# Two mixtures of experts after attention: the held layer in halves, and a phase's comparisons in one step

## The chip, the core and the metric

The kernel runs on one core of a Trainium2 chip. TensorE multiplies, ScalarE and VectorE read its results from PSUM and compute on SBUF, GpSimd does small elementwise work and issues the scatters and gathers by index, and SyncE's queue issues the other DMAs. Each engine runs its own instructions in order and waits for others by semaphores. The metric is device microseconds of one execution, from the runs' median. A profile is of one execution, on the hardware's own clock.

## What is computed

Causal attention with a cumulative bias feeds a first mixture of experts, and this feeds a second one. Cut to the mixtures (N = 1152 tokens, DM = 512, E = 8 experts, hidden width 1024):

```
logits = x @ w_gate                       # first mixture: each token to its best expert
e      = argmax(logits);  gate_w = softmax(logits)[e]
x      = gate_w * (relu(x @ w1[e]) @ w2[e])

logits = x @ w_gate2                      # second mixture: all (token, expert) pairs by falling logit;
for tok, e in descending order:           # a pair counts if the token is free and the expert has room
    if not assigned(tok) and counts[e] < N // E: assign
out[tok of e] = relu(x[tok of e] @ w1b[e]) @ w2b[e]
```

The second mixture's experts hold 144 tokens each. The assignment is found in phases: in each phase every free token points at its best expert that still has room, the kernel ranks the pointing tokens among each other (how many have a larger logit), and an expert that is thereby full closes. The expert that closed in a phase is the next whose weights are loaded.

## The kernel before

**First mixture.** Experts run one after the other, those with few tokens last. Layer 1 of an expert (`layer1`, lines 1004 to 1015) multiplies weights split into a float16 high and a bfloat16 low half with tokens split the same way, three products a term, into PSUM; ScalarE evicts the high half of the hidden values `h`, VectorE subtracts for the low half. Layer 2 follows. Then `back1` turns an expert's results to token rows `xo`, and GpSimd scatters them into `x2d` in HBM.

**The held expert.** The last expert (136 token slots, `HELD`) stops after layer 1. Its contribution to the second mixture's logits comes by a short way (`logits_pe`, `spread_pe`), so that routing can start; its layer 2 is the filler work of TensorE while VectorE routes. It is written as a generator, `held_steps` (from line 1313): each `next` gives 6 matmuls of 136 columns; after the first two of four output blocks (48 matmuls) ScalarE evicts the high half `y` (line 1329), VectorE makes the low half (line 1331), and after the other two (another 48) the same again. Then `rows_steps` transposes both halves of the tokens (line 1348, 16 transposes, 68 tokens a half), ScalarE evicts each (`xo`, `x2f`, line 1350) and GpSimd scatters each (line 1176). `FILL` gives out the steps between the last parts of the first mixture ('f' is a step of the held layer, 'r' one of the rows of the expert before it):

```
FILL = ". rfff rrrff fff"
```

**The first routing phase** is written out by hand behind that. Row maxima `m` are spread over 128 columns by nine transposes (line 1221), evicted by ScalarE as `rowb` (line 1224), and each of nine token tiles is compared with all others (`compare`, a 128 x 1152 comparison): on VectorE (line 1661), or, for the tiles in `act_t`, as a sign on ScalarE (line 1659). TensorE multiplies each comparison with the tiles' expert choice (`products`, line 1667) and so counts ranks. `held_next(n)` takes n steps of the held layer in between:

```
held_next(); ahead(0, 1, 2); held_next(); ahead(4, 3); held_next(8); ahead(5)
held_next(2); ahead(7, 6, 8); head(True); ranked(0, 1, 2, 4, 3); held_next(4); ranked(5, 7, 6, 8)
```

From the ranks VectorE makes `evi` (the number of the first expert that is full, line 1679), for which SyncE's queue waits before it issues that expert's weights (`known`, line 1698, loads at line 128), and `tok` (its token list, line 1715). Then GpSimd gathers that expert's tokens from `x2d` (`gather`, line 1523), which has to wait for all scatters into it. Nine more loads are let go when the gather is issued (`passed`, line 1704). While the weights arrive, ScalarE splits off their high halves (`split_hi`, line 160, `wh`) and VectorE the low ones (`split_lo`, line 164). The tokens left over are packed (line 1804 and the products at line 1806) and the second phase starts. `spread` transposes the gathered tokens (line 1543) and ScalarE and VectorE copy them (line 1548); then layer 1 of the second mixture's first expert begins.

**The second mixture.** Layer 1 has ticks after each group of matmuls and each eviction, layer 2 (`second2`, line 1966) too; a table of scripts says which step of the routing ('w'), which split ('h', 'l'), which half of a gather's spreading or which scatter of results stands at which tick. The generator `phases` yields at each 'w'. In a phase with comparisons (five token tiles, tiles 1 and 4 on ScalarE) one step spreads the row maxima, three steps compare (two tiles each, in the order 0, 2, then 1, 3, then 4), one multiplies and ranks. From the third expert on the first of the three stands at layer 1's first tick and the second at its sixth, so that two evictions (line 1013) and two splits (line 164) of VectorE lie between.

## Time and profile before

| | us |
|---|---|
| median of 3 runs | 436.03 (436.0 to 436.26) |
| profiled execution | 437.73 |
| its span, first to last instruction | 435.9 |
| TensorE busy | 394.1 (90%) |
| VectorE busy | 327.3 (75%) |
| ScalarE busy | 259.1 (59%) |
| GpSimd busy | 189.2 (43%) |
| mean granted TensorE clock | 0.973 |

Busy time is a mean over stages: attention to about 150 us, the first mixture to about 268, the handover with the first routing phase to 297.5, the second mixture behind it. Matmuls are pipelined, so the busy time of one overlaps that of the next; the distance between their starts is their pace. A wait for several semaphores is put down to the one that came last by the profile.

### The profile page before, as it was taken

How to read it: one execution, taken by the hardware profiler on the slowest of the kernel's cores; microseconds unless marked ns; L12 is line 12 of the kernel's file. 1: busy time of each engine (PE TensorE's matmuls, PEld its weight loads, DVE VectorE, ACT ScalarE, POOL GpSimd, SP SyncE). 2: the span in 40 equal slices, each digit the busy share in tenths (PEclk: the TensorE clock that was granted, in tenths of full speed). 3: DMA queues.
4: the chain of work that ended last, by engine and by line, in shares of the span. 5: the costliest groups of instructions: out<-in, count | busy, mean ns of one | idle time of the engine just before them, and what ended most of it. 6: DMA issues, size and time to landing. Idle time of an engine off the chain costs nothing.

```text
span 435.9 us, 13913 instructions
## 1 busy us (share of the span) xinstructions
PE 394.1 (90%) x5359; PEld 365.3 (84%) x5359; DVE 327.3 (75%) x951; ACT 259.1 (59%) x470; POOL 189.2 (43%) x306
## 2 busy tenths in 40 slices
PE   1669999998888799999999999879999999998994
PEld 1447888887767799999999999838999999998993
DVE  7889999989686367868778894776767977977530
ACT  4448888876672356555566742743657695775641
POOL 4387788875870602132044180522043243433131
PEclk9979999999999999999999998968999999999998
DMA  7797989984936989999999390179999797899711
GB/s 145 174 218 182 222 181 212 220 213 147 375 119 201 326 245 321 344 393 344 335 288 384 81 174 5 30 243 312 309 302 378 228 352 267 243 345 284 235 43 36
DMA packets 91327, 103.04 MB, mean 236 GB/s; under 512 B 56136, under 2 KB 59208, under 8 KB 91251
## 3 DMA queue, kind: packets, MB, share of 16 engines
q1 hardware_dynamic: 85859, 91.85, 72.8%
q0 software_dynamic: 4192, 9.91, 7.4%
q8 instruction: 44, 0.72, 0.7%
q10 hardware_dynamic: 1200, 0.30, 0.3%
q14 instruction: 32, 0.26, 0.2%
HBM read 81.42 MB, written 14.59 MB: 220 GB/s over the span
## 4 chain that ended last, share of the span: by engine, by line
PE 57%; DVE 15%; DMA 14%; issue 5%; ACT 3%; POOL 2%; SPq 1%; another core or an unknown queue 1%; POOLq 0%; ACTq 0%; DVEq 0%
PE C L1061 11%; DMA xg<-x2d,tok 8%; PE A L1004 4%; PE A L1006 4%; PE A L1005 4%; PE C L1966 4%; DVE wl L164 4%; PE pog L559 3%; PE pT L452 3%; DMA kf<-in_k_dram 2%; PE pM L476 2%; DVE wf L164 2%; PE A L1966 2%; PE D L1966 2%; DMA wf<-in_moe_w_dram 2%
## 5 line engine op out<-in xcount | busy, mean ns | idle before, releaser
L164 DVE TENSOR_TENSOR wl<-wf,wh 128x1024 bf16<-128x1024 f32 x64 | 78.0, 1233 | 28.6 <-ACT wh L160 27.7
L160 ACT ACTIVATE wh<-wf 128x1024 f16<-128x1024 f32 x64 | 65.8, 1052 | 18.1 <-DMA wf<-in_moe_w_dram 9.7
L1005 PE MATMUL A<-xt,wh 128*128 128x144 f16 (+4 forms) x288 | 61.0, 235 | 0.0
L1006 PE MATMUL A<-xt,wl 128*128 128x144 f16 (+4 forms) x288 | 60.9, 235 | 0.0
L1004 PE MATMUL A<-xt,wh 128*128 128x144 f16 (+4 forms) x288 | 60.9, 235 | 0.0
L1061 PE MATMUL C<-h,wf 128*128 128x160 f32 (+7 forms) x544 | 58.3, 268 | 0.0
L1176 POOL DMA_INDIRECT x2d<-xo,tix x14 | 22.9, 1639 | 74.8 <-DVE l L1193 26.5
L1004 PEld LDWEIGHTS <-wh 128*128 128x128 f16 x512 | 51.0, 100 | 3.3 <-remote 1.7
L1006 PEld LDWEIGHTS <-wl 128*128 128x128 bf16 x512 | 50.9, 99 | 1.9 <-issue 1.7
L1005 PEld LDWEIGHTS <-wh 128*128 128x128 f16 x512 | 50.9, 99 | 0.8 <-issue 0.3
L1990 POOL DMA_INDIRECT out_dram<-x2f,tok x14 | 19.5, 1392 | 54.0 <-ACT h L1012 19.0
L414 POOL TENSOR_TENSOR pl<-pf,ph 128x512 f16<-128x512 f32 x30 | 35.6, 1196 | 10.3 <-DVE ph L403 8.6
L536 ACT ACTIVATE pf<-pE,XB 128x512 f32<-128x512 f32 (+4 forms) x80 | 36.6, 509 | 3.9 <-PE pE L531 3.6
L1061 PEld LDWEIGHTS C<-h,wf 128*128 128x128 f32 x256 | 36.2, 190 | 0.0
L488 DVE CUSTOM_DVE_ANT_0 junk<-pM,cb 128x128 f16<-128x128 f32 (+4 forms) x80 | 32.1, 429 | 4.5 <-PE pM L478 3.8
L164 DVE TENSOR_TENSOR wf<-wf,wf 128x1024 bf16<-128x1024 f32 x28 | 33.4, 1219 | 2.6 <-ACT wf L160 2.6
L1966 PE MATMUL C<-h,wf 128*128 128x144 f16 (+1 forms) x304 | 32.7, 261 | 0.0
L476 PE MATMUL pM<-al,ar 128*128 128x128 f16 (+2 forms) x96 | 26.3, 315 | 7.0 <-DVE rm L488 6.9
L1523 POOL DMA_INDIRECT xg<-x2d,tok x16 | 19.7, 1234 | 24.2 <-DMA x2d<-x2f,tix 6.2
L160 ACT ACTIVATE wf<-wf 128x1024 f16<-128x1024 f32 x28 | 29.3, 1055 | 0.0
L559 PE MATMUL pog<-vf,pf 128*128 128x65 f32 x180 | 28.7, 282 | 0.0
L1004 PE MATMUL C<-xt,wh 128*128 128x144 f16 x128 | 24.6, 226 | 0.0
(431 smaller groups left out, 1180.5 us busy)
## 6 DMA issues: line engine op xcount, KB each, us to landing
wf<-in_moe_w_dram SPq DMA_DIRECT2D x128, 512.0 KB
xd<-zero SPq DMA_DIRECT2D x18, 257.0 KB
cb<-cumd SPq DMA_DIRECT2D x16, 288.0 KB
x2d<-zero SPq DMA_DIRECT2D x9, 260.5 KB
kf<-in_k_dram SPq DMA_DIRECT2D x16, 128.0 KB
vf<-in_v_dram SPq DMA_DIRECT2D x16, 128.0 KB
qf<-in_q_dram SPq DMA_DIRECT2D x14, 128.0 KB
bl<-al SPq DMA_DIRECT2D x16, 72.0 KB
```

The source lines that it names most:

```text
L160: nc.scalar.activation(hi, src, AF.Copy)
L164: nc.vector.tensor_sub(lo, src, hi)
L414: (nc.gpsimd if ENG[name][i % 2] == "P" else nc.vector).tensor_sub(o, x, y)
L476: nc.tensor.matmul(o, AR[m][:, t * P:(t + 1) * P], AL[m][:, j0:j1], start=True, stop=not diag)
L488: nc.vector.tensor_tensor_reduce(junk[:w, :j1 - j0], o, CB[m][:w, j0:j1], 1.0, r if t == 4 and j0 == 0 else -3e38, OP.add, OP.max, r)
L536: nc.scalar.activation(d, o, AF.Exp, bias=x, scale=2.0 ** -13)
L559: nc.tensor.matmul(o, pf[:, c:c + P], VF[n % 4][:, j, h], start=False, stop=j == t)
L1004: nc.tensor.matmul(ph[:, g], wh[:, c, fs], xt[:, c], start=c == 0, stop=False)
L1005: nc.tensor.matmul(ph[:, g], wh[:, c, fs], xt[:, 4 + c], start=False, stop=False)
L1006: nc.tensor.matmul(ph[:, g], wl[:, c, fs], xt[:, c], start=False, stop=c == 3)
L1061: nc.tensor.matmul(py[:, g], a[:, f, d], b[:, f], start=k == 0, stop=k == len(terms) - 1)
L1966: nc.tensor.matmul(py[:, g], a[:, f, d], b[:, f], start=k == 0, stop=k == len(terms) - 1)
```

## The change

The held layer is made in two halves of its tokens instead of two halves of its output blocks. The generator `products` multiplies all four output blocks for 68 tokens, then for the other 68: twice as many matmuls, each with half the columns and 12 to a step instead of 6. High half, low half, the rows' homes in SBUF (`homes`: memset and gate value on GpSimd), the transposes (`turn`) and the copy with its scatter (`put`) are methods that the hand-written order calls one by one. VectorE compares seven of the nine tiles instead of six. In the later phases the three comparisons of VectorE (tiles 0, 2, 3) all stand in the first of the three steps.

```diff
-    def held_steps():
-        for e in HELD:
-            N = CAPS[e]
-            hh, hl = held[e]
-            ys = yh, yl = in_halves(mo1["y"], "y", 4, N)
-            for dp in range(2):
-                py = mo1["py"].tile([P, 2, N], F32)
-                for g in range(2):
-                    wh, wl = split_ws(2 * e)(1, 2 * dp + g)
+    class Held:
+        def __init__(self, e):
+            self.e, self.w = e, CAPS[e] // 2
+            self.ys = in_halves(mo1["y"], "y", 4, CAPS[e])
+            self.py, self.pb, self.xs = {}, {}, []
+        def products(self):
+            hh, hl = held[self.e]
+            for q_ in range(NQ):
+                sl = slice(q_ * self.w, (q_ + 1) * self.w)
+                py = self.py[q_] = mo1["py"].tile([P, 4, self.w], F32)
+                for d in range(4):
+                    wh, wl = split_ws(2 * self.e)(1, d)
                     terms = [x for f in range(8) for x in ((wh, hh, f), (wl, hh, f), (wh, hl, f))]
                     for i, (a, b, f) in enumerate(terms):
-                        nc.tensor.matmul(py[:, g], a[:, f], b[:, f], start=i == 0, stop=i == 23)
-                        if i % 6 == 5:
+                        nc.tensor.matmul(py[:, d], a[:, f], b[:, f, sl], start=i == 0, stop=i == 23)
+                        if i % 12 == 11:
                             yield
-                r = slice(2 * dp, 2 * dp + 2)
-                nc.scalar.activation(yh[:, r], py, AF.Copy, scale=YS)
-                yield
-                nc.vector.scalar_tensor_tensor(yl[:, r], py, YS, yh[:, r], op0=OP.mult, op1=OP.subtract)
-                yield
-            yield from rows_steps(e, ys)
+        def high(self, q_):
+            sl = slice(q_ * self.w, (q_ + 1) * self.w)
+            nc.scalar.activation(self.ys[0][:, :, sl], self.py[q_], AF.Copy, scale=YS)
+        def low(self, q_):
+            sl = slice(q_ * self.w, (q_ + 1) * self.w)
+            nc.vector.scalar_tensor_tensor(self.ys[1][:, :, sl], self.py[q_], YS, self.ys[0][:, :, sl],
+                                           op0=OP.mult, op1=OP.subtract)
+        def homes(self):
+            for q_ in range(NQ):
+                t, g = slots(self.e, q_)
+                xo = mo1["o"].tile([SL, DM + E + 1], F32, name=("xo", "x2f")[q_])[:g.shape[0]]
+                nc.gpsimd.memset(xo[:, DM:DM + E], 0.0)
+                back1_gate(g, xo)
+                self.xs.append((t, xo))
+        def turn(self, q_):
+            pb = self.pb[q_] = pbs.tile([P, 512], F32).bitcast(F16)[:self.w]
+            for k in range(2):
+                for c in range(4):
+                    nc.tensor.transpose(pb[:, (4 * k + c) * P:(4 * k + c + 1) * P],
+                                        self.ys[k][:, c, q_ * self.w:(q_ + 1) * self.w], ident)
+        def put(self, q_):
+            t, xo = self.xs[q_]
+            nc.scalar.activation(xo.bitcast(F16)[:, :2 * DM], self.pb[q_], AF.Copy)
+            back1_out(t, xo)
...
-    head, tiles, compare, products = ranks(pc, m, Bo, Bh0, NTT, (1, 4, 7), 2)
+    head, tiles, compare, products = ranks(pc, m, Bo, Bh0, NTT, (1, 7))
...
-    held_next()
-    ahead(0, 1, 2)
-    held_next()
-    ahead(4, 3)
-    held_next(8)
-    ahead(5)
-    held_next(2)
-    ahead(7, 6, 8)
+    ahead(0)
+    last_held.high(0)
+    last_held.homes()
+    ahead(1)
+    held_next(4)
+    last_held.low(0)
+    ahead(2, 3)
+    last_held.turn(0)
+    last_held.put(0)
+    held_next(4)
+    last_held.high(1)
+    ahead(4)
     head(True)
-    ranked(0, 1, 2, 4, 3)
-    held_next(4)
-    ranked(5, 7, 6, 8)
+    ranked(0, 2, 1)
+    last_held.low(1)
+    ahead(7, 5)
+    last_held.turn(1)
+    last_held.put(1)
+    ranked(3, 4)
+    ahead(6, 8)
+    ranked(7, 5, 6, 8)
...
-                for k in range(3):
-                    gt += [(compare(t), t) for t in tiles[2 * k:2 * k + 2]]
+                for ts in ((0, 2, 3), (1,), (4,)):
+                    gt += [(compare(t), t) for t in ts]
                     yield
```

In the rows of the order below, numbers behind a name tell buffers apart; `g`, `wl_84` and `wh_83` are homes of comparisons, `y` the held layer's result, `m` the row maxima, `mx` the first step after the ranks. VectorE in the first routing phase, before:

```order
L1230 TENSOR_SCALAR Bh_3127<-Bo_3126 128x72
L1661 TENSOR_SCALAR g<-rowb,m_3125 128x1152 x2
L1331 SCALAR_TENSOR_TENSOR y<-C_5155,y 128x2x136
L1661 TENSOR_SCALAR g<-rowb,m_3125 128x1152
L1661 TENSOR_SCALAR wl_84<-rowb,m_3125 128x1152
L1331 SCALAR_TENSOR_TENSOR y<-C_5305,y 128x2x136
L1661 TENSOR_SCALAR wh_83<-rowb,m_3125 128x1152 x2
```

and VectorE in the changed kernel at the same place:

```order
L1230 TENSOR_SCALAR Bh_3127<-Bo_3126 128x72
L1689 TENSOR_SCALAR g<-rowb,m_3125 128x1152
L1339 SCALAR_TENSOR_TENSOR y<-C_5155,y 128x4x68
L1689 TENSOR_SCALAR g<-rowb,m_3125 128x1152 x3
L1339 SCALAR_TENSOR_TENSOR y<-C_5352,y 128x4x68
L1689 TENSOR_SCALAR wl_84<-rowb,m_3125 128x1152
L1689 TENSOR_SCALAR wh_83<-rowb,m_3125 128x1152 x2
```

The first subtraction stands behind one comparison instead of two, there are seven comparisons instead of six, and three instead of two stand behind the second subtraction. ScalarE in the same phase, before (`rowb` ahead, the splitting of weights behind):

```order
L1224 ACTIVATE rowb<-A_5232 128x384
L1329 ACTIVATE y<-C_5155 128x2x136
L1659 ACTIVATE g<-rowb,m_3125 128x1152 x2
L1329 ACTIVATE y<-C_5305 128x2x136
L1659 ACTIVATE wl_84<-rowb,m_3125 128x1152
L1350 ACTIVATE xo<-D_5417 68x1024
L1350 ACTIVATE x2f<-D_5430 68x1024
L160 ACTIVATE wh_83<-wf_78 128x4x256 x2
```

and ScalarE in the changed kernel:

```order
L1224 ACTIVATE rowb<-A_5262 128x384
L1335 ACTIVATE y<-C_5155 128x4x68
L1687 ACTIVATE g<-rowb,m_3125 128x1152
L1359 ACTIVATE xo<-D_5406 68x1024
L1335 ACTIVATE y<-C_5352 128x4x68
L1687 ACTIVATE wl_84<-rowb,m_3125 128x1152
L1359 ACTIVATE x2f<-D_5504 68x1024
L160 ACTIVATE wh_83<-wf_78 128x4x256 x2
```

The first half's rows `xo` moved ahead of the second eviction, and one sign fewer stands between. VectorE at the third expert of the second mixture (`h` the evictions of layer 1, `wf_3047` the low halves of layer 2's weights), before:

```order
L1661 TENSOR_SCALAR g<-rowb,m_6378 128x640 x2
L1013 SCALAR_TENSOR_TENSOR h<-D_6497,h 128x2x144
L164 TENSOR_TENSOR wf_3047<-wf_3038,wf_3047 128x1024 x2
L1013 SCALAR_TENSOR_TENSOR h<-C_6530,h 128x2x144
L1661 TENSOR_SCALAR g<-rowb,m_6378 128x640
```

and in the changed kernel:

```order
L1689 TENSOR_SCALAR g<-rowb,m_6472 128x640 x3
L1013 SCALAR_TENSOR_TENSOR h<-D_6591,h 128x2x144
L164 TENSOR_TENSOR wf_3047<-wf_3038,wf_3047 128x1024 x2
L1013 SCALAR_TENSOR_TENSOR h<-C_6626,h 128x2x144
L1906 TENSOR_REDUCE mx_6750<-px 128x5
```

The third comparison moved ahead of two evictions and two splits; the same holds at the two experts that follow.

## Rows read from the trace of the kernel before

**Rows 1.** Engines by stretch: busy us (instructions), granted clock, DMA share, GB/s.

```profile
core 0: us, PE busy (x) PEld busy (x) DVE busy (x) ACT busy (x) POOL busy (x), PEclk, DMA share, GB/s
289.00:297.50 8.50, 6.12 (x65) 3.58 (x66) 6.36 (x16) 6.73 (x9) 2.32 (x5) 0.70 0.83 257
297.50:331.00 33.50, 33.50 (x445) 33.27 (x444) 24.08 (x99) 17.43 (x30) 10.26 (x14) 0.97 0.99 322
...
296.20:299.60 3.40, 3.40 (x34) 2.85 (x33) 2.86 (x19) 0.64 (x1) 0.50 (x2) 0.50 1.02 361
```

**Rows 2.** Chain of waits in the handover: start, us, what.

```profile
282.69 6.67 DMA x2d<-x2f,tix
...
290.23 4.42 DMA xg<-x2d,tok
```

**Rows 3.** TensorE in time, handover: start, us, line, shapes, count, [idle before, releaser].

```profile
273.37 4.07 PE L1325 MATMUL C<-h,wf 128*128 128x136 f16 x66
...
277.45 0.37 PE L1667 MATMUL A<-Bo,g 128*128 128x8 f16 x9
...
288.85 1.33 PE L1221 MATMUL A<-identf,m 128*128 128x128 f32 x5 [0.86 <-DVE m L1833]
...
294.69 0.43 PE L1543 MATMUL A<-ident,xg 72*128 72x72 f16 x8 [2.38 <-DMA xg<-x2d,tok]
...
297.54 0.33 PE L1004 MATMUL D<-xt,wh 128*128 128x144 f16 x1
```

**Rows 4.** VectorE in time, first routing phase.

```profile
274.33 1.58 DVE L1661 TENSOR_SCALAR g<-rowb,m 128x1152 f16<-128x1152 f32 x2 [1.63 <-ACT rowb L1224]
...
278.08 0.44 DVE L1331 SCALAR_TENSOR_TENSOR y<-C,y 128x272 f16<-128x272 f32 x1 [0.20 <-ACT y L1329]
278.44 1.54 DVE L1661 TENSOR_SCALAR wh<-rowb,m 128x1152 f16<-128x1152 f32 x2
...
284.72 0.16 DVE L1715 TENSOR_SCALAR tok<-s 72x2 int32<-72x2 f32 x1
```

**Rows 5.** ScalarE in time, first routing phase and handover.

```profile
274.99 0.40 ACT L1329 ACTIVATE y<-C 128x272 f16<-128x272 f32 x1 [0.69 <-PE C L1325]
...
280.20 1.01 ACT L1350 ACTIVATE x2f<-D 68x1024 f16<-68x1024 f16 x1
...
290.84 1.06 ACT L160 ACTIVATE wh<-wf 128x1024 f16<-128x1024 f32 x1 [0.46 <-DMA wf<-in_moe_w_dram]
291.80 0.75 ACT L1224 ACTIVATE rowb<-A 128x384 f32<-128x384 f32 x2
...
296.56 0.64 ACT L1548 COPY xt<-A 128x576 f16<-128x576 f16 x1 [0.68 <-PE A L1543]
```

**Rows 6.** SyncE's queue in time: issues of the second mixture's weights.

```profile
283.35 17.12 SPq L128 DMA_DIRECT2D wf<-in_moe_w_dram  x10
```

**Rows 7.** What the DMA moved from 262 to 300 us, 40 slices of 0.95.

```profile
GB/s 1 37 0 0 0 0 17 0 0 0 0 31 127 48 88 9 0 0 0 17 0 0 54 98 199 257 338 345 356 382 276 209 127 169 99 269 405 347 319 375
```

**Rows 8.** TensorE's waits from 296 us: us in total, times, longest.

```profile
PE px L1667 <- DVE g L1661: 1.1, 3, 0.4
```

**Rows 9.** TensorE in time, third and fifth expert of the second mixture.

```profile
339.54 0.27 PE L1667 MATMUL px<-Bh,g 128*128 128x8 f16 x5
340.17 0.28 PE L1667 MATMUL px<-Bo,g 128*128 128x8 f16 x5 [0.36 <-DVE g L1661]
...
374.21 1.94 PE L1966 MATMUL D<-h,wf 128*128 128x144 f16 x20
```

**Rows 10.** VectorE in time, third expert of the second mixture.

```profile
336.57 0.45 DVE L1013 SCALAR_TENSOR_TENSOR h<-D,h 128x288 f16<-128x288 f32 x1
...
339.20 0.45 DVE L1013 SCALAR_TENSOR_TENSOR h<-C,h 128x288 f16<-128x288 f32 x1
339.57 0.55 DVE L1661 TENSOR_SCALAR g<-rowb,m 128x640 f16<-128x640 f32 x1
```

**Rows 11.** ScalarE in time, fifth expert of the second mixture.

```profile
374.83 0.39 ACT L1015 ACTIVATE h<-A 128x288 f32<-128x288 f32 x1
```

More of the change, by code (lines that the diff above doesn't have):

```diff
@@ L1406, in tile_attention_moe_moe @@
     stw.close()
-    todo = {"r": rows_steps(*pend), "f": held_steps(), ".": iter(())}
+    last_held = Held(E - 1)
+    todo = {"r": rows_steps(*pend), "f": last_held.products(), ".": iter(())}
     fill()
```

## The prediction

> **What bounds the kernel now.** I read the stretches by engine first [rows 1]. From 297.5 us to 331 us TensorE is busy in all of its time, so the second mixture of experts is bound by TensorE, and whatever moves the start of its first expert moves the end. From 289 to 297.5 TensorE works 6.12 of 8.5 us: the handover between the two mixtures is where time is lost. Then the chain of waits [rows 2]: the second scatter of the held expert's rows takes 6.67 us to land, and the gather behind it 4.42 us. Then the engines' own order in time. TensorE waits 2.38 us for the gathered rows at 294.69 and begins layer 1 of the first expert at 297.54 [rows 3]. ScalarE converts that expert's weights while they arrive (released by their DMA at 290.84), then makes the row copies at 291.80, and its copy of the gathered tokens at 296.56 waits 0.68 us for TensorE [rows 5]. So two arms meet there: the gather, which ends last, and the weights through ScalarE, which could be 0.68 us later before it decides. Last, TensorE's waits after 297.5 [rows 8]: three waits, 1.1 us in all, for VectorE's third comparison of a phase. One of them is at 340.17; the comparison itself ends at 340.12 because it stands behind two evictions and two weight splits that begin at 336.57 [rows 9, 10].
>
> The profiled execution took 437.73 us with a span of 435.9; the runs' median is 436.03. I make the sum on the span and carry the difference to the median one to one.
>
> **Part 1: the held layer by halves.** It removes 96 matmuls of 136 columns and adds 192 of 68. Now one takes (4.07 - 0.17)/65 = 60 ns [rows 3]; 0.17 is what is left of a single one, from 0.27 for five and 0.37 for nine, which gives 25 ns each [rows 3, 9]. For 68 columns with new weights each time the nearest rows are 8 columns, 25 ns, and the transposes of 72 columns, (0.43 - 0.17)/7 = 37 ns. I take 33, between them and nearer to 72. That is 6.3 us for 5.8: 0.5 us more, half of it in the first half.
>
> The Trainium skill, TensorE: Matmul & The Clock Gate, section Back-to-back issue gap, gives about 81 ns for a sustained pair of weight load and matmul at 128 columns; its section on LDWEIGHTS counts columns over 1.2, so 107 ns for 128. By either, halving the columns would halve nothing and the sum would be that of rival (d). The trace does not agree: 60 ns at 136 columns, 25 ns at 8 with new weights each time [rows 3].
>
> What this does to VectorE decides. Now ScalarE's eviction of the first 48 products starts at 274.99 [rows 5], 0.6 after the 48th matmul (273.37 + 17 x 0.06). VectorE runs six comparisons and two subtractions from 274.33 and ends the last pair at 278.44 + 1.54 = 279.98 [rows 4]. In the changed order it has seven comparisons (ScalarE gives one up) and two stops:
> - first comparison 274.4 to 275.2; the eviction of half one starts about 0.2 later than now, 275.2 + 0.40; the subtraction 0.44, to 276.05;
> - three comparisons at 0.78 (1.58/2), to 278.4. Then it waits: half two needs 96 x 33 ns = 3.2 us of TensorE after 274.7 and the eight transposes of half one, 0.5 us, which stand in between; 278.4, and 0.6 to the eviction: 279.0;
> - eviction 0.40, subtraction 0.44, three comparisons: 282.2.
>
> So the last comparison comes about **2.0 us later** (282.2 - 279.98 = 2.2 with 33 ns, 1.8 with 31), and with it all that follows on VectorE: the expert's number, for which the queue of the weights waits, the token list, now ready at 284.88 [rows 4], and the compaction. The row maxima's transposes, now done at 288.85 + 1.33 = 290.2 [rows 3], come at 292.2.
>
> *The gather.* Half one's rows can be scattered near 279.7, but half two's transposes wait for the subtraction at 279.85; 0.5 of transposes, 0.3 to ScalarE and 1.0 of eviction make 281.6, where now the second eviction ends at 280.20 + 1.01 = 281.2 [rows 5]. The second scatter therefore starts near 282.5, where it is now (282.69). What is gained is its landing: now it shares the DMA engines with the weights from 283.35 on [rows 6], in the change these come 2.0 later. Between the same 6.67 and 1.3 less (the share of the weights, below) the gather starts 0 to 1.3 earlier and its rows are there at 293.4 to 294.7. The token list (286.9) is not in its way. This arm is no later than now.
>
> *The weights.* They are asked for 2.0 later, at 285.35. Upper bound: they land 2.0 later. Lower bound: in the three slices from 283.85 the DMA moved 98, 199 and 257 GB/s, where it reaches 350 after them [rows 7]; without the scatter those slices give back (252 + 151 + 93)/350 x 0.95 = 1.35 us, leaving 0.65. Between them lies the gather, which now comes after the weights and in the change runs among them: 0.3 MB, 0.9 us at 350 GB/s, of which the middle of the range has half. I take 1.3. ScalarE has 0.68 us in hand, so layer 1 starts **0.6 us later** (0 to 1.3). The second scatter's early queueing helps no more than this.
>
> The memsets and gates of the two halves on GpSimd stand behind VectorE's first comparisons as now; ScalarE's copy of half one needs them, and cover is there until 279.0, when the second eviction would be due anyway.
>
> **Part 2: the comparisons in the first step.** Phases 1 to 3 keep VectorE's order, since no other VectorE work lies between their steps. In phases 4, 5 and 6 the third comparison moves ahead of two evictions and two splits: 0.45 us later for these, and TensorE no longer waits. What a wait costs: without it the next product would start 0.025 after the fifth at 339.54 + 0.10 = 339.64, so at 339.67 instead of 340.17, 0.50 us [rows 9]; the row's own 0.36 is the lower figure. Next late is the second layer's low half, which the eviction moved from 339.65 to 340.1 gives, needed at about 340.9: covered. In the third of these places ScalarE's last eviction of layer 1 ends at 374.83 + 0.39 = 375.22 behind a weight conversion that waited for its DMA [rows 11], and the matmuls that read it are the last four of the row at 374.21, near 375.5 [rows 9]: only 0.2 to 0.3 is to be had there. So 0.5 + 0.5 + 0.2 = **1.2 us gained** (0.7 for two at 0.36, 1.5 for three at 0.50).
>
> **Sum:** +0.6 - 1.2 = -0.6, 435.4 us.
>
> **The rivals.** (a) *The weights hardly move.* If they land only 0.65 later, ScalarE's slack takes it, layer 1 starts when it does now, and all three waits go: -1.5, 434.5. For it: the slow first slices; against: the gather in their midst. (b) *The weights follow the expert's number wholly*: +1.3 - 1.2, 436.1. For it: the weights' four parts keep the DMA near 350 GB/s to their end. (c) *As much again at half clock, slower than before.* TensorE was granted 0.50, the lower of its two levels, from 296.2 to 299.6, after its pauses, and layer 1 began in it [rows 1]. If the products come thinner and 2.0 later and as much again is granted half, 3.4 us at half pace cost 1.7: -0.6 + 1.7 = +1.1, 437.1. It decides from a start of layer 1 near 298.5 on, when TensorE's pauses last until then. Against it: the filler products of the handover come later too, and so nearer to layer 1. (d) *A matmul costs its weights*, not its columns: 192 at 60 ns put the first half 96 x 27 ns = 2.6 us further behind and the second 5.2, so the last comparison 7.2 later than now; less 0.7 in the landing and 0.7 in hand, and less 1.2, that is +4.6, 440.6. The 25 ns of the products, with new weights each, speak against it.
>
> That the change does not do what it says can be left aside: the order shows the halves and the moved comparison.
>
> **How the numbers follow.** Forecast 0.40, own range 434.8 to 436.0, three tenths of it under 435.16. (a) 0.28, (b) 0.16, (c) 0.13, (d) 0.03. A measurement of this kernel can tell about 0.2%, 0.87 us, from no change. Faster: 0.28 + 0.12 = 0.40. Same: 0.28 + 0.16 = 0.44. Slower: 0.16. The range of 8 in 10 leaves out (d), the end of (c) and the end of (a): 434.0 to 437.2.
>
> **What would show it.** In the changed profile VectorE's last comparison of the first step ends near 282, the first weight DMA is issued near 285.3, the gather at 289 to 290, layer 1 near 298.1. TensorE's waits for a comparison after 297.5 are gone, and from layer 1's start to the end the span is some 1.2 us shorter. I am wrong if VectorE doesn't stop between the third and fourth comparison of its seven, if layer 1 starts before 297.3 or after 299, or if the three waits come back as waits for ScalarE's evictions.

## The result and the profile after

| | before | changed |
|---|---|---|
| median of 11 runs each, us | 436.26 (434.43 to 438.95) | 440.85 (437.12 to 442.74) |
| ratio | | **1.0085** (1.0056 to 1.0113) |
| profiled execution, us (span) | 437.73 (435.9) | 441.01 (439.2) |

The change makes the kernel 0.85% slower, some 3.7 us, where 435.4 and a range up to 437.2 were forecast. (The ratio is worked out from all the runs; the two medians lie 4.6 us apart.) Runs more than 1.5% above the fastest of their kernel count as slow and are left out of the ratios, and two traces of such runs (the changed kernel's third and that with 48 more transposes, both below) are left out where traces are averaged. The two traces differ by 3.3 us of span, in three stretches: 0.74 lie ahead of the first comparison (275.07 against 274.33), 1.57 between it and the second mixture's layer 1, 1.05 behind that. The first is not the change's: the code there is the same. From 150 to 262 us the same instructions already start 0.9 later in this execution; from 38 to 113 us they started 0.6 earlier. In between lies a stretch of attention in which this execution was granted half the clock (2.4 GHz fell to 1.2) and the other was not. By stretch, with the columns of [rows 1], in the changed kernel and then in the kernel before:

```profile
126.00:130.00 4.00, 4.00 (x35) 3.73 (x35) 2.64 (x7) 2.24 (x5) 2.58 (x3) 0.52 0.32 98
```

```profile
126.00:130.00 4.00, 3.37 (x54) 3.01 (x52) 3.79 (x8) 2.90 (x6) 3.21 (x4) 1.00 0.20 74
```

**The handover.** The changed kernel in time: VectorE's seven comparisons with the two stops, against [rows 4].

```profile
275.07 0.85 DVE L1689 TENSOR_SCALAR g<-rowb,m 128x1152 f16<-128x1152 f32 x1 [1.66 <-ACT rowb L1224]
276.28 0.44 DVE L1339 SCALAR_TENSOR_TENSOR y<-C,y 128x272 f16<-128x272 f32 x1 [0.35 <-ACT y L1335]
276.64 2.40 DVE L1689 TENSOR_SCALAR g<-rowb,m 128x1152 f16<-128x1152 f32 x3
279.35 0.44 DVE L1339 SCALAR_TENSOR_TENSOR y<-C,y 128x272 f16<-128x272 f32 x1 [0.32 <-ACT y L1335]
279.71 0.81 DVE L1689 TENSOR_SCALAR wl<-rowb,m 128x1152 f16<-128x1152 f32 x1
280.44 1.54 DVE L1689 TENSOR_SCALAR wh<-rowb,m 128x1152 f16<-128x1152 f32 x2
...
284.08 0.15 DVE L1707 TENSOR_SCALAR evi<-evf 128x1 int32<-128x1 f32 x1
...
297.16 0.17 DVE L1562 COPY gq<-xg 72x2 f32<-72x2 f32 x1 [0.86 <-DMA xg<-x2d,tok]
```

ScalarE's eviction of the second half, for which the second stop waits:

```profile
278.92 0.40 ACT L1335 ACTIVATE y<-C 128x272 f16<-128x272 f32 x1 [0.41 <-PE C L1329]
```

SyncE's first issue of a weight, against [rows 6], and GpSimd's second scatter and its gather, against [rows 2]:

```profile
285.99 9.05 SPq L128 DMA_DIRECT2D wf<-in_moe_w_dram  x8
```

```profile
282.67 1.11 POOL L1176 DMA_INDIRECT x2d<-x2f,tix  x1 [2.00 <-ACT x2f L1359]
287.80 2.74 POOL L1551 DMA_INDIRECT xg<-x2d,tok  x1 [4.02 <-DVE g L1841]
290.84 1.05 POOL L1551 DMA_INDIRECT xg<-x2d,tok  x1 [0.30 <-issue]
```

TensorE: the held products, the gathered tokens' transposes and layer 1, against [rows 3]:

```profile
274.08 2.88 PE L1329 MATMUL C<-h,wf 128*128 128x68 f16 x84
...
277.24 1.64 PE L1329 MATMUL C<-h,wf 128*128 128x68 f16 x48
...
296.52 0.43 PE L1571 MATMUL A<-ident,xg 72*128 72x72 f16 x8 [2.48 <-ACT g L1687]
...
298.38 0.69 PE L1571 MATMUL A<-ident,xg 72*128 72x72 f16 x8
...
299.85 0.33 PE L1004 MATMUL D<-xt,wh 128*128 128x144 f16 x1
```

Taken from the first comparison on, so that what lies ahead drops out:

| us behind the first comparison | before | changed |
|---|---|---|
| last comparison ends | 5.65 | 6.91 |
| first weight asked for | 9.02 | 10.92 |
| gather issued | 15.90 | 12.73 |
| transposes of its tokens begin | 20.36 | 21.45 |
| layer 1 begins | 23.21 | 24.78 |

The gather leaves 3.2 us earlier and its rows come 1.1 later: 8.7 us pass from its issue to the first transposes, against 4.4 in the kernel before [rows 2]. (The wait of 2.48 is put down to a sign of ScalarE that ended in the same moment; by the trace's landing events the first half's rows were complete at 296.47, the second's at 297.13.)

**Behind layer 1.** TensorE's waits from 299 us, changed kernel, against [rows 8]: us in total, times, longest.

```profile
PE C L2003 <- ACT h L1015: 1.7, 1, 1.7
PE D L1005 <- DVE xt L1576: 0.9, 1, 0.9
PE D L2019 <- ACT y L2009: 0.5, 2, 0.3
PE px L1695 <- ACT g L1687: 0.4, 1, 0.4
PE A L1221 <- DVE xt L1576: 0.4, 1, 0.4
PE D L2003 <- ACT h L1015: 0.4, 1, 0.4
```

The three waits for VectorE's third comparison are gone, as forecast; others of 4.3 us stand there (0.4 of it for a comparison on ScalarE). The kernel before had, beside the 1.1 of [rows 8], one that the forecast did not speak of:

```profile
PE D L1005 <- issue: 1.5, 1, 1.5
```

The longest of the new ones is ScalarE's order: a weight's conversion (`wh`) stands ahead of an eviction (`h`) and waits 3.21 us for its DMA, and TensorE waits for the eviction.

```profile
393.57 1.06 ACT L160 ACTIVATE wh<-wf 128x1024 f16<-128x1024 f32 x1 [3.21 <-DMA wf<-in_moe_w_dram]
394.53 0.39 ACT L1015 ACTIVATE h<-C 128x288 f32<-128x288 f32 x1
```

A second trace of the kernel before (below) takes 139.7 us from layer 1 to the end, where the first takes 138.3 and the changed kernel's two take 139.4 and 139.7. So single traces don't show a loss behind layer 1; what speaks for it are the times of the next section.

### The profile page after: what moved, and what is told of

Its sections match the earlier page's. It is cut to its first block, busy times and chain, and to the rows that moved or that the text cites. A ratio compares the mean times of both kernels' runs of the same rounds, so it can differ in the third digit from the quotient of the medians.

```text
span 439.2 us, 14101 instructions
## 1 busy us (share of the span) xinstructions
PE 399.3 (91%) x5453; PEld 368.5 (84%) x5453; DVE 327.3 (75%) x952; ACT 258.3 (59%) x469; POOL 192.7 (44%) x306
## 4 chain that ended last, share of the span: by engine, by line
PE 60%; DMA 15%; DVE 14%; issue 5%; ACT 3%; SPq 1%; POOL 1%; POOLq 0%; DVEq 0%; ACTq 0%
PE C L1061 11%; DMA xg<-x2d,tok 7%; DMA wf<-in_moe_w_dram 6%; PE A L1004 4%; PE pog L559 4%; PE A L1005 4%; PE A L1006 4%; PE pT L452 3%; PE C L2003 3%; DVE wl L164 2%; PE pM L476 2%; DVE junk L488 2%; PE pE L528 2%; PE pE L529 2%; PE D L2003 2%
## 5 line engine op out<-in xcount | busy, mean ns | idle before, releaser
L2027 POOL DMA_INDIRECT out_dram<-x2f,tok x14 | 19.8, 1413 | 60.8 <-ACT h L1012 26.2
L559 PE MATMUL pog<-vf,pf 128*128 128x65 f32 x180 | 30.1, 292 | 0.0
L1551 POOL DMA_INDIRECT xg<-x2d,tok x16 | 21.5, 1341 | 19.4 <-PE A L1221 5.5
L559 PEld LDWEIGHTS pog<-vf,pf 128*128 128x128 f32 x180 | 25.0, 201 | 0.0
```

Source lines behind the costliest of these rows:

```text
L559: nc.tensor.matmul(o, pf[:, c:c + P], VF[n % 4][:, j, h], start=False, stop=j == t)
```

## Experiments: which part

Theory A: the loss is the first part's. Theory B: the second part costs. **Comparisons alone** takes the kernel before with

```diff
-                for k in range(3):
-                    gt += [(compare(t), t) for t in tiles[2 * k:2 * k + 2]]
+                for ts in ((0, 2, 3), (1,), (4,)):
+                    gt += [(compare(t), t) for t in ts]
```

and **halves alone** takes the changed kernel with these lines the other way round. Both, and both kernels again, on one chip:

> Only the second part: the held layer as before, the later phases' comparisons in their first step. Theory A (the second part gains what the forecast said, three waits of TensorE gone; what was lost lies in the first part): ratio to before 0.9972, 1.2 us less (0.7 to 1.5); TensorE's three waits for VectorE's third comparison are gone and no other wait over 0.3 us stands in their place. Theory B (the second part itself costs: evictions and splits of VectorE and ScalarE 0.45 us later put layer 2 behind, as TensorE's waits for ScalarE at 378 and 395 us in the changed kernel suggest): ratio 1.002 to 1.005, and these waits show here too.

> Only the first part: the held layer in halves and seven comparisons on VectorE, the later phases' comparisons two, two and one as before. Theory A (the loss is the first part's: the expert's number comes 1.9 us later, with it the weights and the gathered rows, and the rest of the weights' stream runs behind): ratio 1.009 to 1.012, the changed kernel's 1.0085 and what the second part gains. Theory B (the second part costs 1 to 2 us of it): 1.002 to 1.005. The layer 1 of the second mixture's first expert begins 2.0 to 2.4 us later than in the trace of before by both.

> The changed kernel a second time. If what its trace shows in the handover is the program's own and not the execution's, TensorE's row maxima transposes again begin within 0.3 us of 273.07, plus or minus what differs before 268 us, the gathered rows again land within 0.5 us behind the fourth weight, and the time stands at 1.0085 of before (1.005 to 1.012). If the long gather (8.7 us from issue to landing) was chance, it takes 4 to 6 us here and the ratio is nearer to 1.002.

> The kernel before a second time, against itself: the ratio is 1.000 within 0.002, or the comparison can't tell the sizes in dispute. By theory A and B alike its trace shows three waits of 0.36 us for the third comparison and the gather landing 4 to 5 us after its issue; if these differ from the first trace, single waits of one trace can't be priced.

| | ratio to before | 95% interval |
|---|---|---|
| comparisons alone | 0.9972 | 0.9945 to 0.9998 |
| halves alone | 1.0048 | 1.0014 to 1.0082 |
| changed, again | 1.0101 | 1.0058 to 1.0144 |
| before, again | 0.9996 | 0.9965 to 1.0028 |

Neither theory holds. The first part loses 0.5% alone, 2.1 us, and the second gains, but together they lose 1.0%: the second part, a gain of 0.28% by itself, stands for a loss of some 0.5% on top of the first. (The intervals of 1.0048 and 1.0101 overlap; this difference is clear of the noise only together with a second one of 0.5%, below.) The long gather repeats: in the second trace of the changed kernel it leaves 12.7 and its tokens are transposed 21.3 us behind the first comparison. Comparisons alone were run twice more, on other chips:

> Only the second part, a second time. If the first look's gain is the second part's own: ratio 0.995 to 0.999 and TensorE's three waits for the comparison gone; its layer 1 to the end takes 136 to 138 us (134.92 in the first trace, which was of the fastest run), and waits of TensorE for gathered tokens or weights add up to under 3 us after layer 1's start. Rival (it was chance): ratio 1.000 or more.

> Only the second part, for comparison on this chip: 0.997 to 1.000 after two looks (0.9972 and 1.0001). Theory L: at least one wait over 1 us at the start of a layer 1 behind the fourth expert in its trace, with the copy of the tokens released late; rival W: such a wait has a weight's landing behind it.

1.0001 (0.9966 to 1.0037) and 0.9960 (0.9932 to 0.9988). TensorE's waits from layer 1 on, in the second and then in the third trace:

```profile
PE C L1005 <- issue: 1.9, 1, 1.9
PE D L1005 <- DVE xt L1548: 1.7, 1, 1.7
PE D L1982 <- ACT y L1972: 0.3, 1, 0.3
```

```profile
PE D L1982 <- ACT y L1972: 0.3, 1, 0.3
```

So the part's own gain is there in all three (no wait for a comparison), and what it comes to goes with waits at the start of a layer 1 that some executions have and some have not: 139.0 us from the first layer 1 to the end with them, 134.9 and 135.2 without, against 138.3 and 139.7 before.

## Experiments: the handover

Theory C: a gather among the weights lands when the four weights ahead of it have landed, whenever it was issued. **Without the second scatter** lets the kernel before gather early; **gather later** lets the changed kernel gather late, and with the gather the nine loads that are let go behind it:

```diff
-            back1_out(t, xo)
+            if e != E - 1 or q_ == 0:
+                back1_out(t, xo)
```

```diff
-    xg = {0: gather(tok[:, 0])}
-    passed(9)
...
     nc.vector.reduce_sum(Lr, pL.rearrange("p c k e -> p c e k"), axis=AX.X)
...
+    nc.gpsimd.tensor_copy(lag, Lr[:, 0, :1])
+    xg = {0: gather(tok[:, 0])}
+    passed(9)
```

> The kernel before, with the second scatter of the held expert's rows left out (those 68 tokens' rows are not written, so their outputs are wrong). The gather needn't wait for its landing: issued some 12.5 us after the first comparison instead of 15.6. Theory C: the weights come as before (the fourth at 19.1 to 19.9), the gathered rows with them at 19.4 to 20.5, and layer 1 begins at 22.8 to 23.2, no more than 0.4 earlier. The forecast's step: rows at 16.9, no longer last, and layer 1 earlier by what the weights allow, 22.5.

> The changed kernel, but GpSimd issues the gather only behind the compaction, some 15.4 us after the first comparison instead of 12.7. Theory C (the gather's rows land when the four weights in front of it have landed, whenever it is issued): its last rows land at 21 to 22 us after the first comparison as in the changed kernel, 6 us after its issue, and layer 1 begins at 24.6 to 25.2. Rival (a gather takes 8.6 us there for a reason of its own): landing at 24 and layer 1 near 27. The forecast's own step (4.4 us from issue to landing): landing at 19.8 and layer 1 below 24.

> The changed kernel with the gather behind the compaction, a second time and timed. Theory C (an early gather runs among the weights and holds them up without landing sooner): layer 1 again begins 23.7 to 24.2 us after the first comparison, where the changed kernel's five traces with the early gather have 24.6 to 25.9, and the ratio to before is 1.003 to 1.006 instead of 1.0085 to 1.011. Rival (the early gather costs nothing of the time, the loss is elsewhere): layer 1 at 24.6 or later, or the ratio stays at 1.008 or more.

Without the second scatter: first comparison, gather, transposes of its tokens, layer 1.

```profile
273.72 1.66 DVE L1662 TENSOR_SCALAR g<-rowb,m 128x1152 f16<-128x1152 f32 x2 [1.55 <-ACT rowb L1224]
```

```profile
286.14 1.69 POOL L1524 DMA_INDIRECT xg<-x2d,tok  x1 [4.29 <-DVE g L1805]
```

```profile
293.45 0.66 PE L1544 MATMUL A<-ident,xg 72*128 72x72 f16 x8 [2.54 <-DMA xg<-x2d,tok]
...
297.04 0.33 PE L1004 MATMUL D<-xt,wh 128*128 128x144 f16 x1
```

Gather later, the second of its two runs, the same:

```profile
274.10 0.83 DVE L1689 TENSOR_SCALAR g<-rowb,m 128x1152 f16<-128x1152 f32 x1 [1.68 <-ACT rowb L1224]
```

```profile
290.25 2.06 POOL L1551 DMA_INDIRECT xg<-x2d,tok  x1 [0.63 <-issue]
```

```profile
294.56 0.43 PE L1571 MATMUL A<-ident,xg 72*128 72x72 f16 x8 [1.52 <-DMA xg<-x2d,tok]
...
297.46 0.33 PE L1004 MATMUL D<-xt,wh 128*128 128x144 f16 x1
```

| us behind the first comparison | gather issued | transposes begin | layer 1 |
|---|---|---|---|
| before | 15.90 | 20.36 | 23.21 |
| before, without the second scatter | 12.42 | 19.73 | 23.32 |
| changed | 12.73 | 21.45 | 24.78 |
| changed, gather later | 16.15 | 20.46 | 23.36 |

In the kernel before, a gather that leaves 3.5 us earlier is there 0.6 earlier, and layer 1 begins no earlier. In the changed kernel one that leaves 3.4 **later** is there 1.0 earlier, and layer 1 begins 1.4 earlier. The traces show both sides of it. In the changed kernel the gather's first row moves 5.3 us after the issue, when 93% of the four weights' bytes have moved; with the gather later 2.8 us after it, in the kernel before 1.8. And the fourth weight, asked for 12.8 us behind the first comparison in both, lands at 21.1 in the changed kernel and 20.5 in its second trace, at 19.5 and 19.8 with the gather later. ScalarE's conversion of the third weight waits for its landing in both, in the changed kernel and then with the gather later:

```profile
293.98 1.06 ACT L160 ACTIVATE wh<-wf 128x1024 f16<-128x1024 f32 x1 [1.12 <-DMA wf<-in_moe_w_dram]
```

```profile
292.46 1.06 ACT L160 ACTIVATE wh<-wf 128x1024 f16<-128x1024 f32 x1 [0.44 <-DMA wf<-in_moe_w_dram]
```

Eight traces with the halves and the early gather have layer 1 at 24.3 to 26.2 (mean 25.2), seven without the halves at 22.5 to 23.5 (mean 23.2), two with the halves and the late gather at 23.4 and 23.9. So of 2.1 us that the handover lost, the early gather made 1.6, and the later weights 0.4. "The early gather" means here the gather with the nine loads behind it, of which the first leaves at 17.7 in the changed kernel and at 20.8 with the gather later; no run moved the one without the other.

Theory C holds without the second scatter and fails in the changed kernel. There a later gather lands earlier, 4.2 and 4.3 us after its issue, as the forecast's own step has it, and layer 1 comes before the 24.6 to 25.2 of theory C: the early gather also holds the weights up. In time this is not shown. The ratio with the gather later is 1.0079 (1.0045 to 1.0113), where 1.003 to 1.006 were wanted, on a chip on which the changed kernel did not run; the changed kernel's own ratios on other chips, 1.0085 and 1.0101, lie within that interval.

Two more runs asked why the first weight is asked for 1.76 us after the expert's number (285.99 less 284.23), and 1.5 to 1.8 in all traces with the halves, but 1.07 to 1.09 in those without. A fetch of 16 KB of instructions falls there, so 16 or 48 more transposes of the identity at the very start, where TensorE waits anyway, move its place in the stream:

```diff
+        for _ in range(0 if padded else 16):
+            nc.tensor.transpose(p[:, :P], ident, ident)
+        padded.append(1)
```

> The changed kernel with 16 more TensorE transposes of the identity at its very start, where TensorE waits until 7.84 us; nothing else moves but the place in TensorE's instruction stream at which 16 KB of instructions are fetched (284.26 us in the changed kernel, in the same moment as SyncE's load of the expert's number, which takes 1.13 us there and 0.45 in the kernel before). Theory F (the fetch holds SyncE up): the load takes 0.45 us here, the first weight is asked for 10.2 us after the first comparison instead of 10.92, layer 1 begins 0.5 to 0.7 earlier (24.0), and SyncE's issue of 1.07 to 1.47 us at 382 is short; the ratio to before is 1.004 to 1.008 instead of 1.0085 to 1.010. Rival (the load is long because of what is in flight, scatters or VectorE's work): the load stays at 1.13 and the ratio at 1.009.

> As the kernel with 16 more transposes, but 48: the fetches stand elsewhere again. Theory F: the load takes 0.45 us here too, and the time differs from the changed kernel's by what SyncE's long issues in the later experts cost, ratio 1.002 to 1.010, with each issue over 0.9 us again beside a fetch. Rival: load 1.13 us, ratio 1.009.

The ratios are 1.0112 (1.006 to 1.0164) and 1.0067 (1.0023 to 1.011), and the delay is 1.75 and 1.77. The run with 16 does not test theory F: the fetch moved by 0.2 us only, from 9.2 to 9.0 behind the first comparison, and still runs beside SyncE's load of the number, which begins at 9.2. With 48 the fetch was over at 8.1, before the load began at 9.2, and the load took 1.14 us all the same. So theory F falls; what holds SyncE up by 0.7 us is open.

## Experiments: the late waits

Why does the second part lose on top of the halves? Theory D: the weights' stream is as late as TensorE. Changed kernel and halves alone with the output scatters cut to 64 of 512 columns:

```diff
+    SHORT = 64
...
-        out2(tok[:, e, q_:q_ + 1], xo)
+        nc.gpsimd.indirect_dma_start(
+            out=dump[:, :], out_offset=bass.IndirectOffsetOnAxis(ap=tok[:, e, q_:q_ + 1], axis=0),
+            in_=xo[:, :SHORT], in_offset=None, bounds_check=NTOK - 1, oob_is_err=False)
```

> The changed kernel, with the second mixture's rows scattered in 64 columns instead of 512 into a spare buffer (most of the output is not written): 0.26 MB of DMA traffic less per expert, some 5 per cent, with the same number of issues. Theory D (behind layer 1 the weights' stream is as late as TensorE, so time that TensorE gains is lost in waits for weights and gathered tokens): TensorE's waits for these from layer 1 to the end, 3.6 to 4.7 us in the changed kernel's traces, fall under 2.5, and the time falls by 1 us or more against the changed kernel; against the same without the second part it is 0.5 to 1.6 us less. Rival O (the second part's order of VectorE's work makes the late waits): it is 0.5 to 2 us more than the same without the second part, as the changed kernel is against the halves alone.

> The halves alone, without the second part, with the same short scatters. Theory D: 0.5 to 1.6 us more than the changed kernel with short scatters, with the three waits of 0.36 us in its trace. Rival O: 0.5 to 2 us less than that.

1.0121 (1.0073 to 1.017) and 1.0074 (1.0041 to 1.0108). TensorE's waits in the trace of the changed kernel with short scatters fell to 2.2 us, under the 2.5 of theory D, but the time did not follow, so theory D falls: with less traffic the second part costs 0.5% on top of the halves again. Each of the two differences is within its noise (0.53 and 0.47%, give or take 0.6); together they come to 0.5%, give or take 0.4. The two traces with short scatters don't show it: both take 137.6 us from layer 1 to the end. The second trace of the changed kernel shows what the wait at the start of a layer 1 is. TensorE, VectorE, GpSimd, and then the stretches behind it:

```profile
383.14 0.42 PE L1571 MATMUL A<-ident,xg 72*128 72x72 f16 x8
383.40 1.23 PE L2003 MATMUL C<-h,wf 128*128 128x144 f32 x8
384.46 0.23 PE L1004 MATMUL C<-xt,wh 128*128 128x144 f16 x1
386.62 0.22 PE L1005 MATMUL C<-xt,wh 128*128 128x144 f16 x1 [1.94 <-DVE xt L1576]
```

```profile
386.11 0.46 DVE L1576 COPY xt<-A 128x576 f16<-128x576 f16 x1 [2.67 <-PE C L2003]
```

```profile
381.87 0.96 POOL L2027 DMA_INDIRECT out_dram<-x2f,tok  x1 [5.05 <-DVE sel L1741]
383.14 1.14 POOL L1551 DMA_INDIRECT xg<-x2d,tok  x1 [0.30 <-issue]
384.58 1.03 POOL L1551 DMA_INDIRECT xg<-x2d,tok  x1 [0.30 <-issue]
```

```profile
299.00:387.20 88.20, 85.56 (x1218) 83.78 (x1217) 67.36 (x233) 55.20 (x91) 31.98 (x33) 0.98 0.91 302
387.20:390.60 3.40, 3.40 (x32) 3.40 (x30) 1.56 (x3) 1.74 (x3) 0.00 (x0) 0.50 1.04 300
```

The second group of transposes of the next expert's tokens ends at 383.56 by the record, but VectorE, which copies them, is released only at 386.1. TensorE, which needs the copy, stands for 1.94 us, and behind that is granted half the clock for 3.4. Such groups give their signal within 0.01 us of their recorded end in most places. The Trainium skill, Perfetto Trace Analysis, section Tensor Engine Instruction, says that the end of a matmul is computed and its signal sent when PSUM has acknowledged all writes; the trace agrees as far as recorded end and signal lie 2.5 us apart here, and so does not tell which of the two is late.

Theory L: this late signal eats the second part's gain. Its cure is to transpose two ticks of layer 2 earlier from the third expert on, so that the copy has time:

```diff
-    THEN = "w h l h l0 w w . . . wh 1l h wl h . w l s tl wh l"
+    THEN = "w h l h l0 w w . . . wh 1l h wl h . ws lt . l wh l"
```

> Only the second part, and in the experts from the third on the two groups of transposes of the next expert's gathered tokens stand two ticks of layer 2 earlier (some 2 us). Theory L (TensorE's signal of the second group comes 0.5 to 2.6 us late in some experts, when GpSimd issues its scatter and gather around it; the copy of the tokens and layer 1 then wait, and this eats what the second part gains): waits at the start of a layer 1 behind the third expert add up to under 0.6 us instead of 1.5 to 4.4, and the ratio to before is 0.993 to 0.997, some 1 us or more below the second part alone on the same chip. Rival W (it is the weights' stream that is late, the wait would only move): the ratio equals the second part alone, and the waits come back for weights.

> The changed kernel with the same earlier transposes. Theory L: 1 to 2 us less than the changed kernel, ratio 1.003 to 1.007, late waits at the start of a layer 1 gone. Rival W: 1.008 to 1.012 as the changed kernel.

> The kernel before with the same earlier transposes and nothing else. Theory L: its one wait of 1.5 to 1.8 us near 399 is gone where it occurs, ratio 0.996 to 0.999, three waits of 0.36 us stay; so the second part is worth 0.5 to 1.2 us on top of it (ratio of the kernel with both below this). Rival W: ratio 1.000.

> The changed kernel with the next tokens' transposes two ticks earlier, beside the changed kernel on the same chip. Theory L: 1 to 2.5 us below the changed kernel (1.0024 of before in the first look, against 1.0085 to 1.011 for the changed kernel on other chips). Rival (the first look's chip was the reason): within 0.8 us of the changed kernel.

> The changed kernel a third time: 1.0085 to 1.011 of before by both theories if chips don't differ in it; its trace has again a layer 1 that starts 24.6 to 25.9 us after the first comparison, a load of the expert's number of 1.13 us, and late waits of 3.6 to 4.7 us in all behind layer 1.

| | ratio to before | 95% interval |
|---|---|---|
| comparisons alone, early transposes | 0.9967 | 0.9935 to 0.9999 |
| before, early transposes | 1.0015 | 0.9986 to 1.0044 |
| changed, early transposes | 1.0024 | 0.9993 to 1.0055 |
| changed, early transposes, other chip | 1.0053 | 1.0022 to 1.0084 |
| changed, third time, that chip | 1.0160 | 1.0117 to 1.0203 |

In the changed kernel theory L holds: on one chip the earlier transposes make 1.0160 into 1.0053, 4.7 us, more than was expected, and the long wait at the start of a layer 1 is gone. (1.0160 is the highest of the changed kernel's three ratios; against 1.0085 and 1.0101, on other chips, the gain is 1.4 to 3.4 us.) TensorE's waits from 299 us there:

```profile
PE D L2019 <- ACT y L2009: 0.8, 2, 0.5
PE C L2003 <- ACT h L1015: 0.5, 1, 0.5
PE px L1695 <- ACT g L1687: 0.4, 1, 0.4
PE C L1005 <- DVE xt L1576: 0.3, 1, 0.3
```

For the kernel before and for the comparisons alone it is wrong: 1.0015 is no gain, and 0.9967 equals the 0.9960 of the comparisons alone on that chip, whose trace had no such wait to lose. TensorE's waits behind layer 1 other than for VectorE's comparisons, without the 0.3 of the last rows: 0.3 to 2.3 us in six traces without the second part; 0.0, 0.2 and 3.6 with it alone; 4.0, 3.3 and 4.4 in the changed kernel (the third of these with 16 transposes more at its start), 2.2 in it with the short scatters, 4.7 and 2.3 with the gather later; 1.9 and 1.7 in it with the earlier transposes. (Comparisons alone with the earlier transposes had one of 2.0, at another place, for a check that VectorE computes.)

The late signal itself can be counted: from the third expert's tokens on each trace has six such second groups. In the six traces with both parts and the old order, two or three signals come more than 0.3 us behind the recorded end. In eight with the old order and one part or none it is none or one, but two in the second trace of comparisons alone. In the four with the earlier transposes it is none. The copy starts up to 2.7 us behind the group there, behind VectorE's splits, and is in time: so the edit works because the signal is no longer late, not because the copy got more time. It also moves the groups away from GpSimd's issues: of the second groups that it moves, all but one have the next gather start 1.9 us or more behind them. Why both parts together meet the late signal more often is not settled. The time at which GpSimd issues its scatter and gather around these transposes differs by tenths of a us between the traces, which may be the reason; no run moved GpSimd's issues alone.

## Why the prediction was wrong, point by point

- **TensorE's price of a half** was right: 84 matmuls of 68 columns in 2.88 us and 48 in 1.64 are (2.88 - 0.17)/83 = 33 and 31 ns; 33 was taken. Rival (d) is out.
- **VectorE's delay** was put too high: 1.26 us at the last comparison, not 2.0 to 2.2. The term that was mis-sized is the 0.6 us between the second half's last matmul and ScalarE's eviction: the matmuls ended 3.8 us behind the first comparison (277.24 + 1.64 less 275.07), where 4.0 was forecast, but the eviction followed 0.04 later (278.92). So the second subtraction began 4.28 us behind the first comparison (279.35 less 275.07) and not 5.1, and VectorE stopped 0.32 for it.
- **The weights' issue** at 1.9 us later met the forecast's 2.0 by two errors: 1.2 from VectorE, and 0.7 that SyncE takes longer between number and issue, which nothing in the trace of before had shown.
- **The gather** is the step that failed in the handover. "... the gather starts 0 to 1.3 earlier and its rows are there at 293.4 to 294.7. ... This arm is no later than now": it started 3.2 earlier behind the first comparison, 2.4 of it since the scatter's landing took 4.25 us (282.67 to 286.92 by its landing events) without the weights beside it, not 6.67; but it then ran among the weights, took 8.7 us instead of 4.4, and with its loads held them up. The sum charged the weights for the gather (half of 0.9 us) and never the gather for the weights. The trace of before gave a hint: the gather, issued at 290.23, had its first half there at 294.64 by its landing events, 0.45 behind the fourth weight (294.19).
- **Layer 1**: 0.6 later was forecast, up to 1.3; 1.57 in the first two traces, 2.1 in the mean of all. With the gather late it would have been right (0.4).
- **Part 2**: the three waits went in every trace, and comparisons alone gained 1.2, 0 and 1.7 us where 1.2 was forecast. The step that failed is that nothing was asked of what comes late next except layer 2's low half. The trace of before had a wait of 1.5 us that ends at 399.06, for the copy of the next tokens, and there too the signal to the copy came 2.1 us late. In the changed kernel the new waits, 4.0 and 3.3 us in its two traces, are more than the 1.1 us that went; half the clock followed them in one of the two. That TensorE finds the copy late because it comes earlier is not shown: two of the three traces of comparisons alone have no such wait.
- **The rivals**: the side was that of (c), 437.1, and its condition came true in part. From the first comparison through the handover the half clock lasted 10.2 us in both of the first two traces, but 14.5 in the mean of the eight with the halves and the early gather (10.2 to 20.5) and 10.2 in the mean of eight without the halves (6.8 to 13.7). Behind the start of layer 1, where (c) priced it, it lasted 2.2 us in the mean of either group; what the rest cost ahead of layer 1 no run tells. The measured 440.85 lies next to the 440.6 of (d), by luck: its price of a matmul was wrong. (a) and (b) asked only how far the weights follow the number.

**What beats the kernel before**, by little, is the second part alone: 0.9972, 1.0001 and 0.9960 in three comparisons on three chips, of which the second shows no gain; weighted by their intervals they come to 0.9974, give or take 0.0017.

## What to carry to other kernels

A transfer that is let go early among large ones has two prices, what it waits and what it makes wait; a row that shows it alone prices neither. Before a chain is cut short, look at which queue its next step joins, and test the step by delaying it: a later issue that lands earlier shows the price. And a wait that is taken from a bound engine is a gain only as far as the next thing that it needs is there in time: the trace before had one place where it was not.

## What was unexpected of the hardware

- A gather of 72 rows took 4.4 us behind the weights and 8.7 among them, and issuing it 3.4 us later, with the loads behind it, made it land 1.0 earlier. The Trainium skill, DMA: Bandwidth & Descriptors, section Queues, rings and completion order, says that each DMA engine takes turns between its queues packet by packet; by that an early gather would have passed most of the weights, and here it did not: its first row moved when 93% of their bytes had. Whether it stood in a queue until then or was not yet made up, no run tells.
- TensorE's signal to VectorE came 2.5 us behind the recorded end of the transposes, and up to 3.2 in other traces; transposing two ticks earlier, away from GpSimd's issues, brought it back to 0.01.
- SyncE's first issue came 1.5 to 1.8 us behind the expert's number in the kernels with the halves and 1.07 to 1.09 in the others, and moving an instruction fetch away from the load of the number (48 transposes) did not change it.
